# Fewer and longer unread matmuls at the start, and one batch's value products one slot later

## The chip, the cores and the metric

One core of one Trainium2 chip. The metric is device time in microseconds (us). Kernels are compared only within the same rounds.

## The reference

Sliding-window causal attention (window 64), then a mixer: a low-rank product over the sequence and an MLP with ReLU, all added to the attention's output.

```python
B, H, S, D = 8, 8, 576, 64
scores = (q @ k.T) / sqrt(D)                  # only 0 <= i - j < 64 is kept
x = softmax(scores) @ v                       # -> (B, S, 512)
u = x + ((x.transpose(0, 2, 1) @ U) @ V).transpose(0, 2, 1)     # U: 576 x 32, V: 32 x 576
out = u + relu(u @ w_ch1) @ w_ch2             # 512 -> 2048 -> 512
```

Inputs and output are float32; the kernel computes in bfloat16 with float32 accumulation.

## The kernel before

All engines get a hand-written order. Batch 0's attention runs alone at the start. Then the MLP of chunk `c` (512 tokens) is a list of 32 slots: slots 0 to 15 are the first product (psA, four 512-column matmuls each, L724), slots 16 to 31 are quarters of the second product (psU, four matmuls each, L748). Pieces of the next batch's attention are hung behind slots.

The kernel opens with matmuls whose result nobody reads, to keep TensorE busy until the first data arrives (the first transposes of k start at 6.22 us):

```python
unread = psum["spare"].tile([P, CH], FP32, name="unread", tag="spare")

def turn_over(n, cols, rows=P):
    for _ in range(n):
        nc.tensor.matmul(                                   # L829
            unread[0:rows, 0:cols], idle[:, 0:rows], idle[:, 0:cols], start=True, stop=True
        )

turn_over(62, 96)
# ... (cut) batch 0's attention: transposes of k and q (K, Q; L281), biases (B; L335), scores (S; L345), first values (L; L407)
order = "K0 K1 B0 B1 Q0 Q1 S0 K2 S1 K3 B2 Q2 Q3 S2 B3 S3 L0 B4 S4 L1"
# ... (cut) values of batch 0 (L407), transposes of x (XT; L583), x-with-U products (U; L531, and L539 for the last tile),
#     the last quarter of XT (X3), hh-with-V products (HT; L590), then the MLP of chunk 0
```

Batch 1's attention hangs behind chunk 0's slots:

```python
PLACE_1 = {
    "T": [11, 11, 12, 12, 14, 14, 15, 15],
    "S": [12, 13, 15, 16, 16],
    "M": [13, 14, 16, 17, 17],
    "SV": [18, 18, 19, 19],      # copies that shift v by half a tile (ACT L148, DVE L151)
    "PV": [20],                  # values: 72 short matmuls (L407), then DVE scales them into xs (L488, L498, L510)
    "U": [25],                   # U products of all of xs into pshh (L531, L539)
    "V": [26, 31],
    "UT": [28, 29, 30, 31, 102],
}
```

For batch 1 the first U product reads the tile of xs that the last scaling instruction (L510) writes.

The softmax here doesn't subtract the row's maximum and nothing guards it: scores larger than these inputs give would overflow.

## Time and profile before

| | before |
|---|---|
| median of 3 executions known when predicting (all 6 later) | 313.06 us (312.84) |
| span of the profiled execution | 311.4 us |
| PE busy | 303.9 us, 98% |
| first psA matmul (end of the start) | 21.80 us |
| first value matmul of batch 1 | 45.90 us |
| first U product of batch 1 | 51.61 us |

From the page of the kernel before: busy time by engine, and the chain of work that ended last, with shares of the span by engine and by line.

```profile
PE 303.9 (98%) x2897; PEld 148.4 (48%) x2919; DVE 161.8 (52%) x308; ACT 108.8 (35%) x173; POOL 101.7 (33%) x133
...
PE 93%; DMA 3%; POOL 2%; issue 1%; ACT 0%; DVE 0%; POOLq 0%
```

A kernel whose PE is busy 98% of the time can change only where PE is not, or where its work changes. PE's idle time lies in the first 22 us: it is busy for 18.83 of them, and for 283.71 of the 285 that follow. There are two places there to look at. In the timeline of the start, each line gives start and length in us, engine, source line, operation, tiles, shape, count, and in brackets the idle time of the engine before it and what ended it. PEld is the weight load that goes ahead of each matmul (2,919 loads and 2,897 matmuls on the page).

```profile
1.26 5.03 PE L829 MATMUL unread<-idle 128*128 128x96 bf16 x62 [1.26 <-DVE idle L155]
6.22 0.45 PE L281 MATMUL tpg<-ident,kr 96*64 96x96 bf16 x12
...
13.30 0.45 PEld L345 LDWEIGHTS <-kf 64*64 64x64 bf16 x18 [0.42 <-issue]
13.30 0.58 PE L345 MATMUL sc<-qf,kf 64*64 64x128 bf16 x18
...
18.51 0.68 DVE L418 TENSOR_TENSOR xs<-xr,rcpr 64x512 bf16<-64x512 f32 x1
...
19.97 0.10 PEld L539 LDWEIGHTS <-ub 128*32 128x32 bf16 x4 [0.66 <-issue]
19.97 0.29 PE L539 MATMUL psh<-xs,ub 128*32 128x256 bf16 x4 [0.36 <-issue]
...
20.31 0.65 ACT L546 CAST hh<-psh 128x256 bf16<-128x256 f32 x2 [2.82 <-PE psh L539]
...
21.80 0.59 PE L724 MATMUL psA<-uTc,w1b 128*128 128x512 bf16 x2 [0.40 <-ACT uTc L599]
```

L539 needs the xs that DVE finished at 18.51 + 0.68 = 19.19 us, yet even its weight load, which waits for nothing, starts at 19.97: the page calls such time "issue", a wait that no semaphore explains.

The second place is batch 1's values and what hangs on them. From the timeline between 43 and 54 us:

```profile
43.87 1.67 ACT L148 COPY vB<-vA 64x520 bf16<-64x520 bf16 x3
...
45.06 0.33 DVE L151 COPY vB<-vA 64x520 bf16<-64x520 bf16 x1 [0.24 <-DMA vA<-in_v_dram]
...
45.90 0.22 PE L407 MATMUL xw<-vA,pts 128*64 128x65 bf16 x1
...
47.17 0.18 DVE L487 RECIPROCAL rce<-xe 128x4 f32<-128x4 f32 x1 [1.78 <-PE xe L407]
...
50.48 0.86 DVE L510 TENSOR_TENSOR xs<-one,rco 64x256 bf16<-64x256 f32 x2
...
51.61 0.62 PE L531 MATMUL pshh<-xs,ub 128*32 128x512 bf16 x8
```

The copies that the values need end at 43.87 + 1.67 = 45.54, before the values start at 45.90. DVE is done with xs at 51.34, PE comes to U at 51.61: 0.27 us of slack.

### The profile page before, as it was taken

Reading aid. Unit: us, or ns where it says so; the run is one execution under the profiler, and the core shown is the slowest. Engines: PE = TensorE matmul, PEld = TensorE weight load, DVE = VectorE, ACT = ScalarE, POOL = GpSimd, SP = SyncE. Lnnn points to the kernel's source line nnn. Section 1 sums busy time; section 2 is a strip of 40 time slices with the busy share of each in tenths; the row PEclk is TensorE's granted clock in tenths of the full one; section 3 lists DMA queues with packets and bytes.
Section 4 is the critical chain, followed back from the end, with each engine's and each line's share of the span. In section 5 each row is a group of like instructions: output and inputs, shape, how many; then the busy total and the mean of one; then the engine's idle time right before and its main releaser. Section 6 shows DMA issues by size and latency. Waiting matters only on the chain.

```text
span 311.4 us, 6970 instructions
## 1 busy us (share of the span) xinstructions
PE 303.9 (98%) x2897; PEld 148.4 (48%) x2919; DVE 161.8 (52%) x308; ACT 108.8 (35%) x173; POOL 101.7 (33%) x133
## 2 busy tenths in 40 slices
PE   8989999999999999999999999999999999999996
PEld 7643554544455544453445344544454444444443
DVE  4665467437758753774368435844574343016011
ACT  3745670467038510642063304340345003201500
POOL 8693263293497097029308710000000000000000
PEclk9999999999999999999999999999999999999999
DMA  7999999999999999999999999515100545010012
GB/s 108 167 210 208 205 168 147 145 148 154 129 150 140 126 152 156 182 161 159 163 155 207 150 106 181 128 48 133 69 2 0 120 180 193 27 76 34 0 64 73
DMA packets 156496, 39.88 MB, mean 128 GB/s; under 512 B 145040, under 2 KB 151440, under 8 KB 156464
## 3 DMA queue, kind: packets, MB, share of 16 engines
q0 software_dynamic: 104720, 18.88, 87.3%
q1 hardware_dynamic: 51744, 20.55, 35.0%
q8 instruction: 23, 0.38, 0.5%
q14 instruction: 9, 0.07, 0.1%
HBM read 37.97 MB, written 9.44 MB: 152 GB/s over the span
## 4 chain that ended last, share of the span: by engine, by line
PE 93%; DMA 3%; POOL 2%; issue 1%; ACT 0%; DVE 0%; POOLq 0%
PE psA L724 41%; PE psU L748 40%; DMA vA<-in_v_dram 3%; PE sc L345 3%; PE xw L407 2%; PE psv L619 2%; PE pshh L531 1%; PE tpu L653 1%; PE tpg L281 0%; POOL qr L119 0%; PE low L345 0%; PE psh L531 0%; POOL vB L151 0%; PE xr L407 0%; POOL kr L119 0%
## 5 line engine op out<-in xcount | busy, mean ns | idle before, releaser
L724 PE MATMUL psA<-uTc,w1b 128*128 128x512 bf16 (+1 forms) x580 | 131.2, 378 | 0.4 <-ACT uTc L599 0.4
L748 PE MATMUL psU<-w2b,c 128*128 128x512 bf16 (+2 forms) x572 | 127.5, 373 | 1.3 <-issue 0.3
L748 PEld LDWEIGHTS <-c 128*128 128x128 bf16 x592 | 56.0, 98 | 66.4 <-issue 3.6
L724 PEld LDWEIGHTS <-w1b 128*128 128x128 bf16 x580 | 54.1, 98 | 64.4 <-issue 2.9
L736 ACT ACTIVATE c<-psA 128x512 bf16<-128x512 f32 x84 | 50.0, 597 | 88.3 <-PE psA L724 88.0
L761 DVE TENSOR_TENSOR osb<-psU,un 128x512 f32<-128x512 f32 (+2 forms) x29 | 19.5, 672 | 69.3 <-PE psU L748 69.3
L734 DVE TENSOR_SCALAR c<-psA 128x512 bf16<-128x512 f32 x60 | 41.3, 688 | 25.6 <-PE psA L724 25.6
L634 DVE TENSOR_TENSOR un<-psv,xs 128x512 bf16<-128x512 f32 (+3 forms) x48 | 26.1, 592 | 23.5 <-PE psv L619 23.3
L365 ACT ACTIVATE pts<-sc 128x1024 bf16<-128x1024 f32 x32 | 31.4, 1028 | 2.3 <-PE sc L345 2.3
L137 POOL DMA_DIRECT2D vA<-in_v_dram x32 | 28.5, 915 | 8.1 <-DMA w1b<-in_moe_w_ch_dram 2.8
L128 POOL DMA_DIRECT2D qr<-in_q_dram x30 | 26.7, 890 | 4.5 <-DMA w2b<-in_moe_w_ch_dram 3.1
L128 POOL DMA_DIRECT2D kr<-in_k_dram x30 | 26.7, 890 | 4.1 <-PE psA L724 2.0
L398 ACT ACTIVATE ptl<-low 128x256 bf16<-128x256 f32 x6 | 2.3, 384 | 62.0 <-PE high L345 62.0
L371 DVE TENSOR_TENSOR pts<-pts,maskA 128x1024 bf16<-128x1024 bf16 x28 | 19.1, 682 | 1.7 <-ACT pts L365 1.7
L922 POOL COPY held<-qf 1x1 bf16<-1x1 bf16 x5 | 1.1, 228 | 54.0 <-DMA qf<-qr 54.0
L498 DVE TENSOR_TENSOR xs<-xw,rcw 128x896 bf16<-128x896 f32 x14 | 15.3, 1091 | 0.5
L345 PEld LDWEIGHTS <-kf 64*64 64x64 bf16 x704 | 9.9, 107 | 7.7 <-issue 7.0
L345 PE MATMUL sc<-qf,kf 64*64 64x128 bf16 (+1 forms) x608 | 11.7, 212 | 0.5 <-DVE qf L298 0.3
L407 PEld LDWEIGHTS <-pts 128*64 128x64 bf16 x512 | 9.9, 110 | 3.7 <-issue 3.2
L546 ACT CAST hh<-pshh 128x512 bf16<-128x512 f32 x7 | 4.1, 586 | 13.7 <-PE pshh L539 13.5
L656 ACT COPY uTc<-tpu 128x512 bf16<-128x512 bf16 x9 | 5.3, 585 | 10.2 <-PE tpu L653 10.2
L407 PE MATMUL xw<-vA,pts 128*64 128x65 bf16 x217 | 8.4, 195 | 0.0
(115 smaller groups left out, 175.3 us busy)
## 6 DMA issues: line engine op xcount, KB each, us to landing
out_dram<-osb SPq DMA_DIRECT2D x27, 256.0 KB, 2.3
vA<-in_v_dram POOLq DMA_DIRECT2D x32, 128.0 KB, 8.1
kr<-in_k_dram POOLq DMA_DIRECT2D x24, 128.0 KB, 5.8
qr<-in_q_dram POOLq DMA_DIRECT2D x24, 128.0 KB, 6.4
w2b<-in_moe_w_ch_dram POOLq DMA_DIRECT2D x4, 512.0 KB, 15.0
out_dram<-late SPq DMA_DIRECT2D x8, 256.0 KB, 3.0
vB<-in_v_dram POOLq DMA_DIRECT2D x8, 128.0 KB, 12.3
w1b<-in_moe_w_ch_dram POOLq DMA_DIRECT2D x2, 512.0 KB, 11.5
```

Source lines behind the costliest of these rows:

```text
L128: nc.gpsimd.dma_start(out=dst[0:rows, t, :, :], in_=src[b, :, t * P : t * P + rows, :].rearrange("h p d -> p h d"),)
L137: nc.gpsimd.dma_start(out=dst[:, :, 0:D], in_=v[b, :, lo : lo + P, :].rearrange("h p d -> p h d"))
L345: nc.tensor.matmul(sc[g][r0 : r0 + W, col * W : (col + n) * W], keys_of(j, u, rs), queries_of(j, blk, n, rs), start=not spare, stop=last o ...
L365: nc.scalar.activation(out=dst, in_=sc[:], func=ACT.Exp, scale=scale)
L371: nc.vector.tensor_tensor(out=dst, in0=dst, in1=maskA.rearrange("p g n w -> p g (n w)"), op=ALU.mult)
L407: nc.tensor.matmul(dst, pts[:, h // 2, h % 2, blk, :] if blk < NB - 1 else ptl[:, h // 2, h % 2, :], rhs, start=True, stop=True,)
L634: nc.vector.tensor_tensor(out=u_tiles[g][rs, cs], in0=ps[0][n][rs], in1=x[rs, t, :, :].rearrange("p h d -> p (h d)")[:, cs], op=ALU.add,)
L724: nc.tensor.matmul(ps[i][:, ts.start * P : ts.stop * P], w1b[:, dc, i * P : (i + 1) * P], uTc[:, ts, dc, :], start=(dc == 0), stop=(dc == ...
L734: nc.vector.tensor_relu(out=c1[i][:], in_=ps[i][:])
L736: nc.scalar.activation(out=c1[i][:], in_=ps[i][:], func=ACT.Relu)
L748: nc.tensor.matmul(acc[t][:, lo:hi], c1[i][:, t * P : (t + 1) * P], w2b[:, i, lo:hi], start=(i == 0), stop=(i == NFC - 1),)
L761: nc.vector.tensor_tensor(out=osb[:, lo:hi], in0=acc[t][:, lo:hi], in1=u_tiles[g][:, lo:hi], op=ALU.add,)
```

## The change

Its intent, as far as the edit tells: the unread matmuls keep their total of columns (62 x 96 = 5952, 50 x 119 = 5950) in fewer instructions, and batch 1's copies and values get one slot more for v to land.

```diff
-        "SV": [18, 18, 19, 19],
-        "PV": [20],
+        "SV": [19, 19, 20, 20],
+        "PV": [21],
         "U": [25],
 ...
-    turn_over(62, 96)
+    turn_over(50, 119)
```

The two programs differ on PE only: 24 instructions fewer at the start (12 weight loads and 12 matmuls), and four psU matmuls move from behind the values to before them. The order on DVE, ACT, POOL and SP is the same.

## The prediction

> **What bounds it now.** TensorE. Busy share by engine: PE 98%; the chain of waits is 93% PE, its two MLP products alone 81%. From 27 us on, the PE timeline is dense: starts of successive 512-column matmuls are 0.215 us apart, and the few larger gaps are missing records. Only the first 22 us have real PE idle time. So only three places can move the total: the start, the switch to batch 1's values (45.9 us), and what hangs on those values.
>
> **Change 1, the unread matmuls.** In the timeline 62 matmuls of 96 columns run 1.26 to 6.2 us, starting 80 ns apart until the clock is released at 6.03 us. [...] My estimate for 119 columns is 99 ns, so 50 take 4.96 us, as 62 did: the clock and the first transposes should not move. What changes is the count: 24 fewer PE instructions (12 loads, 12 matmuls), and nothing else there.
>
> That may matter. At 19.97 us the last U product (L539) starts 0.75 us after the weight load before it, although its values were ready at 19.19 (DVE timeline); the profile says "issue", 0.36 us on the chain. It is row 703 of the PE program[...]. [...] 23 instruction packets of 16,384 bytes for about 5,860 PE instructions. I read the gap as PE waiting for its next block after a burst of short matmuls. With 24 fewer instructions, row 703 becomes the first MLP weight load, where PE waits 0.4 us for the uTc copies anyway. Gain: about 0.4 us, first MLP matmul at 21.4 instead of 21.8.
>
> **Change 2, batch 1's values one slot later.** The copies keep their order on ACT and DVE. On PE four psU matmuls (0.86 us) move from behind the 72 value matmuls to before them. In the timeline values start at 45.90; last copies they need end at 45.54, so before had about 0.4 us of margin and no wait to remove. But U (L531) stays in slot 25 and needs all of x: DVE scales from 47.17 to 51.34 (last L510), and U starts at 51.61. Values to end of DVE is 5.5 us; values to U is 5.7 us of PE work before, 4.85 after. So PE will wait about 0.65 us for DVE at U. PE is dense afterwards, so nothing gives this back.
>
> **Sum.** -0.4 at the start, +0.65 at U, of which a possible 0.1 us wait for the last w2b block (landing 47.73 us, needed at about 47.65) is inside: net +0.25 us. 313.06 + 0.25 = 313.3 us; 80% range 312.7 to 313.9. Chances: faster by over 2%: 0.003; within 2%: 0.99; slower by over 2%: 0.007.
>
> **Signs.** Right: unread still ends near 6.2 us; no "issue" gap before L539 (starts near 19.55); first psA near 21.4; values (xw) near 46.4; a new PE wait of 0.5 to 0.65 us before pshh, put down to DVE L510, U near 51.9; afterwards all shifted by one constant. Wrong: the L539 gap stays (it is not the instruction count), or U has no wait.
>
> **What would make it wrong.** If the gap at L539 is not instruction supply, the loss is 0.65 (313.7). If in unprofiled executions batch 1's v lands later than in this trace, before already waits at its values, and the later slot wins that back (312.7 or so). If the clock is released later with the new matmuls, the start slows, though until 16.07 us the chain runs through the v loads and POOL copies, which hide up to 0.3 us.

The sum: -0.4 at the start and +0.65 at U make +0.25 us, and 313.06 + 0.25 = 313.3 us. But the -0.4 rests on reading the gap at row 703 as the end of a block of instructions, and for that I had only one gap and the packets: 23 of them for about 5,860 instructions, so 255 to a packet. The 99 ns for 119 columns are an estimate that follows from the 80 ns of the trace: 80 x 119 / 96.

## The result, and the profile after

| | before | after |
|---|---|---|
| median of 6 executions, us | 312.84 (312.72 to 313.33) | 314.06 (313.72 to 314.39) |
| span of the profiled execution, us | 311.4 | 312.0 |
| first psA | 21.80 | 21.78 |
| first value matmul of batch 1 | 45.90 | 46.74 |
| first U product of batch 1 | 51.61 | 52.25 |

Ratio 1.0036, 95% interval 1.0023 to 1.0049. In us it is 0.0036 x 312.84 = 1.13. The change is slower by that much, and the predicted +0.25 us with a range up to 313.9 did not hold it.

From the page of the kernel after:

```profile
PE 303.5 (97%) x2885; PEld 147.6 (47%) x2907; DVE 162.6 (52%) x308; ACT 108.8 (35%) x173; POOL 101.4 (32%) x133
...
PE 94%; DVE 2%; DMA 2%; issue 1%; ACT 1%; POOLq 0%
```

DVE is new on the chain with 2%, and POOL has left it. The start, in the timeline of the kernel after:

```profile
1.26 4.51 PE L829 MATMUL unread<-idle 128*128 128x119 bf16 x50 [1.26 <-DVE idle L155]
6.13 0.45 PE L281 MATMUL tpg<-ident,kr 96*64 96x96 bf16 x12 [0.35 <-DMA kr<-in_k_dram]
...
13.21 0.39 PE L345 MATMUL sc<-qf,kf 64*64 64x128 bf16 x13
...
14.25 0.25 PE L345 MATMUL sc<-qf,kf 64*64 64x128 bf16 x5 [0.65 <-issue]
14.25 0.11 PEld L345 LDWEIGHTS <-kf 64*64 64x64 bf16 x4 [0.81 <-issue]
...
19.75 0.12 PEld L539 LDWEIGHTS <-ub 128*32 128x32 bf16 x4
19.77 0.47 PE L539 MATMUL psh<-xs,ub 128*32 128x256 bf16 x4
...
21.78 0.59 PE L724 MATMUL psA<-uTc,w1b 128*128 128x512 bf16 x2 [0.40 <-ACT uTc L599]
```

The gap before L539 is gone, as predicted. But the 18 scores at 13.2 us are now torn in two, with 0.8 us of "issue" in between. The chain of waits no longer runs through the v loads and POOL copies until 16 us: it runs through this gap. So the first psA came at 21.78 and not at 21.4.

Batch 1's values, in the timeline of the kernel after:

```profile
43.85 1.67 ACT L148 COPY vB<-vA 64x520 bf16<-64x520 bf16 x3
...
46.74 0.22 PE L407 MATMUL xw<-vA,pts 128*64 128x65 bf16 x1
...
48.02 0.18 DVE L487 RECIPROCAL rce<-xe 128x4 f32<-128x4 f32 x1 [2.65 <-PE xe L407]
...
51.34 0.86 DVE L510 TENSOR_TENSOR xs<-one,rco 64x256 bf16<-64x256 f32 x2
51.59 0.09 PEld L531 LDWEIGHTS <-ub 128*32 128x32 bf16 x1 [0.42 <-issue]
52.25 0.61 PE L531 MATMUL pshh<-xs,ub 128*32 128x512 bf16 x8 [0.58 <-DVE xs L510]
```

PE is at U at 51.59, loads its weights, and has to wait for DVE until 52.25: 0.66 us, put down to DVE L510. This is the predicted wait and the predicted size.

That explains 0.6 us, the difference of the two spans, and not 1.13. The profiled execution after (313.72) was also the fastest of its six; the other five lay between 314.01 and 314.39. So something at the start or later costs 0.3 to 0.7 us more in the other executions than in this one.

**Theory.** PE's instructions arrive in blocks, and PE waits where it comes to the end of one before the next is there. The size of a block is an estimate, about 255: the traces show 23 instruction packets for about 5,860 instructions (255 each), and the two gaps stand 254 rows of the PE program apart, in before at row 703 (L539, 0.75 us) and in after at row 449 (0.91 us; in before 0.16 us at that row), in the middle of the scores that start at 13.3 us. (One wait instruction between them is not counted as a row, so 254 rows are 255 instructions.) The ends of the blocks would then stand at fixed rows, near 448 and 703. Taking 24 instructions out at the start moves both block ends to other work. **Rivals:** the width of the unread matmuls or the moment of the clock's release makes the start slower; or the loss is all from the new slot; or some later wait differs.

### The profile page after: what moved, and what is told of

It reads as the page before. It is cut to its first block, busy times and chain, and to the rows that moved or that the text cites. A ratio compares the mean times of both kernels' runs of the same rounds, so it can differ in the third digit from the quotient of the medians.

```text
span 312.0 us, 6946 instructions
## 1 busy us (share of the span) xinstructions
PE 303.5 (97%) x2885; PEld 147.6 (47%) x2907; DVE 162.6 (52%) x308; ACT 108.8 (35%) x173; POOL 101.4 (32%) x133
## 4 chain that ended last, share of the span: by engine, by line
PE 94%; DVE 2%; DMA 2%; issue 1%; ACT 1%; POOLq 0%
PE psA L724 41%; PE psU L748 39%; PE sc L345 3%; PE xw L407 2%; PE psv L619 2%; DMA kr<-in_k_dram 2%; PE pshh L531 1%; PE tpg L281 1%; PE tpu L653 1%; DVE xs L498 1%; PE sc L335 1%; PE tpm L281 0%; PE low L345 0%; PE psh L531 0%; DVE xs L418 0%
## 5 line engine op out<-in xcount | busy, mean ns | idle before, releaser
L656 ACT COPY uTc<-tpu 128x512 bf16<-128x512 bf16 x9 | 5.3, 585 | 10.2 <-PE tpu L653 10.2
L761 DVE TENSOR_TENSOR late<-psU,un 128x512 f32<-128x512 f32 x8 | 5.3, 688 | 5.8 <-PE psU L748 5.7
```

Source lines behind the costliest of these rows:

```text
L761: nc.vector.tensor_tensor(out=osb[:, lo:hi], in0=acc[t][:, lo:hi], in1=u_tiles[g][:, lo:hi], op=ALU.add,)
```

## The experiments

Twelve runs were made, eleven new kernels and the change once more. All gave correct results. "Gap" in this section is the time between the starts of two successive weight loads in the trace, 447 to 449 or 701 to 703 of the PE program. Each trace has every weight load of its program (2,919 in before, 2,907 in after), in the program's order, so the rows can be counted. Within the 18 scores that hold row 449, the other loads of the trace of after follow at 0.003 to 0.04 us. The start and length of the instruction packets are in the trace's DMA records: 23 packets of 16,384 bytes in queue 8, for about 5,860 PE instructions (22 in the kernel with 12 unread matmuls). That a packet is the block whose end shows the gap is inferred from the order in time; no run moved a packet alone.

### The unread matmuls alone

```diff
-    turn_over(62, 96)
+    turn_over(50, 119)
```

> 50 unread matmuls of 119 columns, batch 1's values in their old slot. Theory (blocks of PE instructions: the gap falls on PE program row 448 and on 703/704, whatever stands there): an issue gap of 0.7 to 1.0 us in the scores at row 448 near 13.4 us, no gap before L539, no wait at pshh; first psA near 21.8; time +0.1 to +0.6 us over before. Rival (column width or clock release makes the start slower): the gap would stay at L539 and the loss would come before 9 us.

Measured: 314.05 us, ratio 1.004 (1.0022 to 1.0058); span 311.9. The gap at row 449 was 0.83 us, none before L539, first psA at 22.32, no wait at pshh (U at 52.12). The gap, in this kernel's timeline:

```profile
13.84 0.39 PE L345 MATMUL sc<-qf,kf 64*64 64x128 bf16 x13
14.78 0.25 PE L345 MATMUL sc<-qf,kf 64*64 64x128 bf16 x5 [0.56 <-issue]
```

The place of the gap is the theory's. The time is not: +1.0 us by the medians, where +0.1 to +0.6 was expected. The first psA is 0.5 us later than I expected: this execution lost at the start what the profiled execution of the change did not. The two executions share a PE program up to slot 20, so the start itself varies from one execution to the next.

### The slot alone

```diff
-        "SV": [18, 18, 19, 19],
-        "PV": [20],
+        "SV": [19, 19, 20, 20],
+        "PV": [21],
```

> 62 unread matmuls of 96 columns as before, batch 1's values one slot later. Theory: gap before L539 stays (about 0.75 us between weight loads at row 703), PE waits 0.6 to 0.7 us at the first pshh for DVE L510, time +0.65 us over before. Rival (the slot is free or helps; the whole loss is from the unread matmuls): time as before within 0.2 us.

Measured: 313.75 us, ratio 1.0047 (1.0012 to 1.0082; one of six runs took 317.27 at a granted clock of 0.988, so the medians, +0.70 us, say more). The wait at U, in this kernel's timeline:

```profile
51.42 0.09 PEld L531 LDWEIGHTS <-ub 128*32 128x32 bf16 x1 [0.42 <-issue]
52.08 0.61 PE L531 MATMUL pshh<-xs,ub 128*32 128x512 bf16 x8 [0.58 <-DVE xs L510]
```

0.66 us again. The rival that the slot is free falls. But a part of my expectation missed: the gap at L539 was not there (0.03 us), although the program is that of before up to slot 18. The first psA came at 21.61, earlier than in the trace of before.

### Fewer, but not wider

```diff
-    turn_over(62, 96)
+    turn_over(50, 96)
```

> 50 unread matmuls of 96 columns: the instruction count of after with the width of before; old slot. Count theory: gaps as in e1 (row 448 yes, L539 no) and a time within 0.3 us of e1. Rival (width): gaps and time as before (gap at L539, none at row 448).

Measured: 314.19 us, ratio 1.003 (1.0018 to 1.0042). The unread matmuls end a microsecond earlier and are of the old width, and yet:

```profile
14.78 0.25 PE L345 MATMUL sc<-qf,kf 64*64 64x128 bf16 x5 [0.88 <-issue]
```

The gap is at the same row as in the change, ends at 14.78 us as with the 50 wide ones alone, and the first psA is at 22.32 again. Width is not the cause.

This execution also had something new at 101 us: DVE's first vB copy took 0.71 us. DVE's two later copies then started at 102.88 us (102.42 with the unread matmuls alone), and PE paused 0.38 us among the values that need them. The profile puts this pause down to "issue", so that it was the copies is a reading. The first fence is this kernel's timeline, the second that of the unread matmuls alone.

```profile
100.80 0.88 POOL L137 DMA_DIRECT2D vB<-in_v_dram  x1 [0.16 <-issue]
...
101.05 0.71 DVE L151 COPY vB<-vA 64x520 bf16<-64x520 bf16 x1
```

```profile
99.97 0.95 POOL L137 DMA_DIRECT2D vB<-in_v_dram  x1
...
101.02 0.28 DVE L151 COPY vB<-vA 64x520 bf16<-64x520 bf16 x1
```

The copy took 0.28 us where POOL had just finished issuing a load, and 0.71 us where it began within the issue. The slow copy ended at 101.76, 0.08 us after the issue (100.80 + 0.88 = 101.68). Others did alike: in the 14 traces the 15 such copies that started in the first 0.25 us of a POOL issue took 0.27 to 0.28 us, within it, and the 24 that started later in one all ended 0.08 to 0.19 us after its end, ten of them after more than 0.5 us (the profile's spans on POOL are rough). In the trace of after, one started 0.16 us into the issue at 44.15 us and took 0.28 us; the next started 0.36 us into it and took 0.65 us. The traces show that the two meet; what holds the copy is not shown. The five times of this kernel stand in two groups (313.59 twice, 314.19 to 314.20 three times), so I took this meeting as a second suspect for the missing 0.3 us.

### The old count, half of it wider

```diff
-    turn_over(62, 96)
+    turn_over(31, 119)
+    turn_over(31, 73)
```

> 31 unread matmuls of 119 columns and 31 of 73: the count and the columns of before, half of them as wide as after's; old slot. Count theory: as before: gap at L539, at most 0.2 us at row 448, time within 0.2 us of before. Rival (width): part of e1's loss.

Measured: 312.89 us, ratio 1.0001 (0.9989 to 1.0013): as before. No gap at row 449. At L539 the gap was 0.25 us and not 0.75; the first psA at 21.61. So the time follows the count, and the gap of 0.75 us that I had built the gain on is not in every execution of the 62.

### The change again, and with batch 3's copies earlier

```diff
 # the second kernel: the changed kernel, and
-    PLACE_3 = {**PLACE, "SV": [5, 5, 6, 6]}
+    PLACE_3 = {**PLACE, "SV": [4, 4, 5, 5]}
```

> The changed kernel once more, for a second trace and more times. Theory: about 314.05 us in most executions because DVE's first vB copy of batch 3 (near 101 us, 0.28 us alone) meets a POOL load issue and takes about 0.7 us, which PE then waits for at batch 3's values (0.3 to 0.4 us); 313.7 in executions without that meeting. If this trace has a span of 312.3 or more, it shows a DVE copy of 0.6 us or more near 101 us or a larger gap at row 448; if neither is there, the theory of this 0.3 us falls.

> The changed kernel with batch 3's vB copies one slot (0.86 us) earlier, its values where they were. Theory (the copy that meets the POOL issue costs the typical execution 0.3 us): 313.7 us, 0.3 us under the changed kernel of the same rounds, and no PE wait near 102.8 us. Rival (the missing 0.3 us is elsewhere, as at the start): same time as the changed kernel.

Measured: 314.34 us (ratio 1.0034, 1.0002 to 1.0066; one run of 318.83 us is left out of the ratio) and 314.43 us (1.0034, 1.0008 to 1.0061), in a session with outliers (before: 312.66 to 315.14). Moving the copies gained nothing. (In its trace the moved copy met another POOL issue and took 0.58 us, but early enough that PE did not wait.) The second trace of the change has the larger span (312.5), and in it the DVE copy near 101 us took 0.28 us: no meeting. What it has is a larger loss at the start: its first transposes, waiting for k, started at 6.57 us and not at 6.13, its first packet came 0.50 us later, the gap at row 449 was 0.98 us, and the first psA came at 22.29. Of the two alternatives set down before, it is the larger gap; and the second kernel ran as its rival said. So the theory of the meeting falls as the cause of the 0.3 us: a wait of PE after such a meeting near 101 us is seen in one trace only. The other cause stands: the change's first trace was a lucky start.

### Many fewer, and a few more

```diff
-    turn_over(62, 96)
+    turn_over(12, 496)     # the first of the two kernels
+    turn_over(72, 83)      # the second
```

> 12 unread matmuls of 496 columns (5952 columns as before, 100 fewer PE instructions); old slot. Theory: the block ends still stand on PE program rows 448 and 703/704, now batch 0's value matmuls of xr near 14.8 us and deep in the first MLP product; gap at row 448 of 0.3 to 0.9 us, part of it hidden by the wait for the POOL copies near 16.1; no gap at L539; time within 0.4 us of before. Rival (any fewer and longer is worse): worse than the 50 by as much again, 315.

> 72 unread matmuls of 83 columns (5976 columns, 20 more PE instructions); old slot. Theory: the second instruction packet starts as early as before or earlier (10 to 11 us), no gap over 0.3 us at row 448 that PE does not wait out anyway at S3, a gap of 0 to 0.7 us at row 703, now in the U products of tiles 2 and 3 near 18.5 us; time 312.6 to 313.4. Rival (width): 0.2 to 1 us faster than before, the opposite way of the change.

Measured for 12: 315.63 us, ratio 1.0066 (1.0037 to 1.0095), which is +2.1 us; but five of its six executions ran at a granted clock of 0.989 to 0.995. The one at full clock, which is the traced one, took 314.27 us, 0.8 us over the median of before. Whether the 12 wide matmuls bring the lower clock is not shown. Measured for 72: 314.19 us, ratio 1.002 (0.9997 to 1.0043), +0.6 us, unclear. The gap of each, one line of each timeline:

```profile
16.57 0.19 PE L407 MATMUL xh<-vA,pts 128*64 128x65 bf16 x1 [1.45 <-issue]
```

```profile
19.76 0.28 PE L583 MATMUL uam<-ident,xs 128*128 128x128 bf16 x2 [0.82 <-issue]
```

With 12, row 449 is a value matmul of batch 0, and the gap is 1.67 us: larger than expected, and only partly hidden. In that trace the first psA came at 22.98 us, later than in any trace of 62 or 50. So "within 0.4 us of before" missed in the one full-clock execution, while the rival's 315 is met only by executions at a lower clock. With 72, row 703 is a transpose of x, and the gap is 1.21 us, larger than the 0 to 0.7 us expected; the time missed the 312.6 to 313.4 expected as well. In both, the row was the theory's; only the sizes were not. The rival "wider is worse" also needs the 72 to be faster than before, and they were not. In the traces both directions lose at the start (first psA at 22.98 and 22.66), as if what counts is the work that stands at the block ends; by the times, neither loss is clear of noise and clock.

### Values two slots later, and one slot earlier

```diff
-        "SV": [18, 18, 19, 19],
-        "PV": [20],
+        "SV": [20, 20, 21, 21],     # the first of the two kernels
+        "PV": [22],
+        "SV": [17, 17, 18, 18],     # the second
+        "PV": [19],
```

> 62 unread matmuls of 96 as before, batch 1's values two slots later (22). Theory: the wait before the first pshh is 5.5 us of values and DVE less the PE work between, so one slot more adds one slot's 0.86 us: 1.5 us of PE wait, put down to DVE L510; time +1.3 to +1.5 us over before. Rival (a one-time cost of any move): a wait and a loss as with one slot, 0.65 us.

> 62 of 96 as before, batch 1's values one slot earlier (19). Theory: no wait at pshh; instead PE waits 0.2 to 0.6 us inside the values for the vB copies, whose v lands at about 45 us whatever PE does; time +0.1 to +0.5 us over before. If it is faster than before by 0.2 us or more, the old slot was already too late for U.

Measured for two later: 315.67 us, ratio 1.0088 (1.007 to 1.0106), +2.75 us. More than the 1.5 us expected. Its timeline:

```profile
47.74 1.02 PE L748 MATMUL psU<-w2b,c 128*128 128x512 bf16 x4 [0.95 <-DMA w2b<-in_moe_w_ch_dram]
...
54.20 0.61 PE L531 MATMUL pshh<-xs,ub 128*32 128x512 bf16 x8 [1.46 <-DVE xs L510]
```

The wait at U grew to about 1.5 us as expected. The rest is another wait: with the values behind slot 22, slot 22 itself comes before 47.7 us, and it needs the last block of w2b, which had not landed. The values had been covering that load.

Measured for one earlier: 313.43 us, ratio 1.0009 (0.9994 to 1.0024): not clear of noise in four executions (+0.43 us by the medians). The values started at 45.04 us and did not wait for v as I had expected; U came at 51.75.

Together with the other runs this gives a simple relation. From the first value matmul to U it took 5.50 or 5.51 us in all five traces of the values in a later slot (slot 21 in four, slot 22 in one): DVE's time. It took 5.71 us with the values in slot 20 (5.95 once, where PE waited for w2b in between) and 6.71 us in slot 19: PE's own time.

### A few fewer

```diff
-    turn_over(62, 96)
+    turn_over(58, 103)
```

> 58 unread matmuls of 103 columns (5974 columns, 8 fewer PE instructions); old slot. Theory: row 703 falls in the transposes of the last quarter of x, behind which PE waits for hh anyway, so no gap that costs there; row 448 in the scores of S3, gap 0 to 0.5 us if the second instruction packet starts before 11.2 us, 0.7 to 1.0 us if it starts after 11.6 as with 50; time within 0.3 us of before in the first case, +0.5 in the second.

Measured: 313.21 us, ratio 1.0009 (0.9992 to 1.0026): as before. The second packet started at 10.89 us and the gap at row 449 was 0.44 us. At row 703 there was a gap of 0.65 us in the last transposes of x, where it cost nothing. The first psA came at 21.39 us, which is where I had predicted it for the change. A shorter start, but no measurable gain in time.

### The change's matmuls, with the count restored

```diff
-    turn_over(62, 96)
+    turn_over(50, 119)
+    turn_over(12, 8)
```

> The changed kernel's 50 unread matmuls of 119 columns, then 12 more of 8 columns, so that the PE program has the count of before again; old slot. Count theory: second instruction packet starts at 10.2 to 11.0 us, gap at row 448/449 at most 0.3 us, first psA 21.6 to 21.9, time within 0.3 us of before although the 12 extra matmuls make the first transposes up to 0.5 us later. Rival (the 119 columns themselves): gap of 0.8 us or more at row 448, psA at 22 or later, +0.9 us as with 50 alone.

Measured: 313.05 us, ratio 1.0001 (0.9987 to 1.0015), span 311.0. Gap at row 449: none. First psA at 21.43, a little before the 21.6 to 21.9 expected. The 18 scores are whole again:

```profile
1.26 4.94 PE L829 MATMUL unread<-idle 128*128 128x119 bf16 x62 [1.26 <-DVE idle L155]
...
13.23 0.42 PE L345 MATMUL sc<-qf,kf 64*64 64x128 bf16 x18
```

(The view merges the 50 and the 12 into one line of 62 and shows the shape of the first.) The same 50 wide matmuls cost nothing when 12 narrow ones bring the PE program back to its old length. So it is the count, shown by adding it back and by taking it away without the width.

### All traces side by side

"Packet" is the first (for row 703 the second) 16,384-byte packet in queue 8. "End" is the start of the first weight load after the gap. All in us.

| unread matmuls | packet 1 | gap at row 449, end | packet 2 | gap at row 703, end | first psA |
|---|---|---|---|---|---|
| 12 x 496 | 13.28 to 14.79 | 1.67, 16.58 | 20.24 to 21.13 | deep in the MLP | 22.98 |
| 50 x 119, the change | 11.61 to 12.67 | 0.91, 14.25 | 17.92 to 18.85 | hidden | 21.78 |
| 50 x 119, the change again | 12.11 to 13.18 | 0.98, 14.76 | 18.44 to 19.38 | hidden | 22.29 |
| 50 x 119, with early copies | 11.82 to 12.96 | 0.88, 14.51 | 18.29 to 19.23 | hidden | 22.04 |
| 50 x 119, old slot | 12.18 to 13.32 | 0.83, 14.78 | 18.43 to 19.38 | hidden | 22.32 |
| 50 x 96, old slot | 12.22 to 13.31 | 1.15, 14.78 | 18.50 to 19.44 | hidden | 22.32 |
| 58 x 103 | 10.89 to 12.02 | 0.44, 13.70 | 17.60 to 18.55 | 0.65, 20.00 | 21.39 |
| 62 x 96, before | 10.94 to 11.90 | 0.16, 13.47 | 17.64 to 18.57 | 0.75, 19.97 | 21.80 |
| 62 x 96, two slots later | 10.88 to 11.82 | 0.31, 13.47 | 17.49 to 18.42 | 0.78, 19.92 | 21.75 |
| 62 x 96, one slot later | 10.45 to 11.44 | 0.00 | 17.38 to 18.32 | 0.03 | 21.61 |
| 62 x 96, one slot earlier | 10.47 to 11.43 | 0.00 | 17.52 to 18.47 | 0.02 | 21.81 |
| 31 x 119 and 31 x 73 | 10.23 to 11.30 | 0.00 | 17.31 to 18.26 | 0.25, 19.78 | 21.61 |
| 50 x 119 and 12 x 8 | 10.41 to 11.38 | 0.00 | 17.30 to 18.23 | 0.12, 19.51 | 21.43 |
| 72 x 83 | 10.46 to 11.44 | 0.03 | 17.46 to 18.44 | 1.21, 19.75 | 22.66 |

"Hidden" means that this row is the first weight load of the MLP, where PE waits for uTc anyway (0.40 us before psA in the trace of the change).

Three things are to be seen. First, every gap over 0.4 us ends 1.3 to 1.8 us after the end of its packet, whatever work stands there: 14.25 - 12.67 = 1.58, 19.97 - 18.57 = 1.40, 16.58 - 14.79 = 1.79. Second, the first packet starts at 10.2 to 10.9 us with 58 or more unread matmuls, at 11.6 to 12.2 with 50, and at 13.3 with 12. At that moment PE stood between rows 290 and 380 in every trace. That the fewer instructions make PE reach a given row later explains only a part: it passed row 191, about where the estimate puts the block end before, at 8.35 us on the mean of the five traces with 50 and at 7.98 with 62, while the packet started at 11.99 and at 10.56. Third, in all five traces with 50 the first psA comes 7.53 us after the end of the gap at row 449, whatever the gap's size and whenever it ended; in the six with a count of 62 the distance varies from 7.74 to 8.33 us. So with 50 the start hangs on that block end, and with 62 on something else.

## Why the prediction was wrong

**The step that failed** is "Gain: about 0.4 us, first MLP matmul at 21.4 instead of 21.8" (-0.4 in the sum). The reading of the gaps, blocks of about 255 PE instructions and a wait at their end, held: every such gap (0.44 to 1.67 us) fell on one of these rows, though in four of the six traces with a count of 62 neither row has one of more than 0.25 us. But I applied it to one block end and did not move the other.

- I named row 703 and checked what would stand there after the change. The block end before it, at row 448, stands in the scores of 13.3 us. In before it cost 0.16 us there and the page's line showed it only as 0.58 us for work of 0.42. With 24 instructions fewer, the packet for that block came 0.7 to 1.3 us later (11.61 to 12.22 for 10.94), and the gap became 0.83 to 1.15 us in all five traces with 50. Of that, the start lost about half a microsecond: the mean first psA is 22.15 us in the five traces with 50 (21.78, 22.32, 22.32, 22.29, 22.04) and 21.67 us in the six with a count of 62 (21.80, 21.61, 21.61, 21.75, 21.81, 21.43). The term was +0.48 and not -0.4.
- The 0.4 us that I meant to win is not lost in every execution: of the six traces with 62, two have a gap of 0.75 us or more at row 703 and four have 0.25 us or less. I read one trace as if it were every execution.

**What was right.** "PE will wait about 0.65 us for DVE at U": it waited 0.66 us in the slot alone and in each trace of the change, and 5.50 us from values to U was predicted as 5.5. "The old slot had margin and no wait to remove" held too: no trace with slot 20 shows PE waiting for v at the values, and even slot 19 did not.

**The sum.** +0.48 at the start and +0.65 at U make +1.13 us; measured 1.13. That the two agree to the last digit is luck: the first term is a mean over traces of which one was taken per kernel.

**What stays open.** Alone, the unread matmuls cost a ratio of 1.004, which is 1.25 us, where the trace shows 0.5; the 50 narrow ones cost 1.003. The intervals reach down to 0.7 and 0.6 us, and such extras as PE's pause after the DVE copy that met a POOL issue (0.38 us, seen once) may fill the rest, but no run shows it. So the two parts of the change don't add up exactly in time (1.25 + 0.7 against 1.13), while they nearly do in the traces. What decides the start of the packet, and why it varies by 0.5 us between the two traces of the change and by 0.7 us among the kernels with 62, is not shown by these traces either.

The clock's release can be left out as the cause. It is seen where matmuls of one form start to follow faster: in the trace of the change those of 119 columns started 100 ns apart until 4.91 us and 52 to 53 ns apart after it. (Before their release those of 96 columns started 80 ns apart, those of 496 columns 413 ns.) It came at 4.91 us in the trace of the change and at 4.55 in its second trace, whose first psA was 0.5 us later; in the four traces that open with the same 62 matmuls it came at 5.1 to 6.0 us; it came at 7.21 with the unread matmuls alone, and at 7.08 us with 31 and 31, which ran as before.

## What to carry to other kernels

Where a burst of short instructions meets "issue" time that no wait explains, count the instructions. Here such places lay 254 rows apart (449 and 703), and taking 24 instructions out upstream moved other work to both of them at once: the gap before L539 went from 0.75 us to nothing, the one in the scores grew from 0.16 to 0.91. So every such place has to be checked, not only the one that hurts. Here filler work held the program in phase: with 12 matmuls of 8 columns more, the trace shows no gap at row 449, and without them 0.83 us. So keep the count when changing the size, or look at all such places again. And before moving a producer, compare its path to the consumer (5.50 us here) with the work left in between (5.71 before, 4.85 after): slack of one trace against the size of one slot.
